# Token weights turned in two halves, and DMA-turned k copied by VectorE, in an attention and phase-MLP kernel

## The chip, the core and the metric

The kernel runs on one core of a Trainium2 chip. The metric is the device time of one execution in microseconds (us). Engines are called TensorE (PE, with its weight loads PEld), VectorE (DVE), ScalarE (ACT), GpSimd (POOL) and SyncE (SP); here SP's queue issues every DMA.

## What is computed

Two modules follow each other. The first, for 8 batches and 8 heads of 576 tokens with 64 features, adds an attention over tokens pooled by four (144 of them) to an attention in a band of seven tokens:

```python
q_d = q.reshape(B, H, Sd, factor, D).mean(axis=3)      # k_d and v_d likewise, factor 4
out_up = np.repeat(sm_attn(q_d, k_d, v_d), factor, axis=2)
mask = np.abs(pos[:, None] - pos[None, :]) < factor
scores = np.where(mask, scale * np.matmul(q, k.transpose(0, 1, 3, 2)), -1000000000.0)
return out_up + np.matmul(softmax(scores), v)
```

The second takes its result as x, with 512 features:

```python
theta = x @ w_theta
zr, zi = x * np.cos(theta), x * np.sin(theta)
y = np.einsum('ts,bsd->btd', w_tok_r, zr) + np.einsum('ts,bsd->btd', w_tok_i, zi)
u = x + y
return u + np.maximum(u @ w_ch, 0.0)
```

The token weights w_tok_r and w_tok_i are 576 by 576 each and mix tokens: output token t, input token s.

## The kernel before

The work of a batch is cut into steps, each a Python generator's turn; a string of letters, ORDER (L80), says in which order the steps of all batches are emitted, and `pin` (L683) keeps that order on every engine. A letter stands for the next step of its kind: L and v load q, k and v; C and w cast them to bf16; A turns q and k; B pools v; Q and S are pooled and band scores; N and V are pooled and local outputs; T turns the attention output to feature-major x; H gives sine and cosine of theta; Z makes z; X mixes tokens; R is the channel matmul; O is the last sum and the store. The letters l, c and W load, cast and turn the token weights (l and c the theta weights too), h and g load and cast the channel weights. D is warm-up: six matmuls of 512 columns on zeros. The letters q, t, x, z and u are DMA transposes on SP. In the text, X4.4 is step 4 of batch 4's mix, and so on.

PSUM is used as two rings: `w2` (L73) has two buffers, for q and k turns, scores and attention outputs; `w1` (L76) has four, for everything else. A step's matmuls start once the buffer's reader of two or four uses before has run.

Token weights: `weight_loads` (L220) loads five row blocks (four of 128 rows, one of 64) of w_tok_r and then five of w_tok_i. `weight_casts` (L239) casts in the same order, r on GpSimd, i on VectorE. `weight_turns` (L256) has nine steps: step j turns one block of 128 input tokens for all 576 output tokens by five TensorE transposes (the last step has ten, for the 64-token tails of r and i), and one copy of 576 columns, on ScalarE or VectorE by turns, brings it into WT.

Mix: `mix` (L615) has for each of four feature blocks dc nine matmuls of 512 columns (output tokens 0 to 511; L626) and an add on VectorE (L627), and then a tail step of 36 matmuls of 64 columns (L632) with one add (L634).

Turned q and k: for batches 6 and 7 (`DMA_QK`, L288) SP's DMA transposes turn q and k (`turn_qk`, L290), and the turned block lies in SBUF; for the others TensorE turns them into PSUM (L332). In `turns` (L315) each of the four steps of a batch then makes two copies, which also put the tokens into their order (L334): its source takes 9 tokens 128 elements apart for each run of 9 written. All are ScalarE's, but for turned k of batches 6 and 7, which GpSimd copies. VectorE pools by four after it (L342). GpSimd's other work is the casts of q, k and v (L124, L131), the band masks (L445, L447), the pooled-v product (L359), and the x sums of batches 6 and 7 (L545).

Of the kernel before, what the change touches and what calls it, by code (L numbers as in the profile page):

```python
# [9 lines left out]
FP32 = mybir.dt.float32  # L10
BF16 = mybir.dt.bfloat16
AF = mybir.ActivationFunctionType
ALU = mybir.AluOpType
AX = mybir.AxisListType

P = 128
B = 8
H = 8
S = 576
# [22 lines left out]
HALF = 64  # L42
# [5 lines left out]
def kernel(  # L48
# [11 lines left out]
    nc = tc.nc  # L60
# [15 lines left out]
    def w1(name, dt=FP32):  # L76
# [1 line left out]


    ORDER = (  # L80
        "LLLCLLCCCLLLvvvAAvKKKCLCvLCCLLlwLLDKwAwAwwSSQvSVCCBCcllCLllLQcVllNNvvvANcvwTTCCCCAcwSllllSHlccVwwVDV"
        "TTcwATAHHHZZHLSQcDcBccDSLLLLLcCCDCLvWQSZWWNzCLCLvVwCWCCvvvWWSWNZWWVLLwwwwAXVAXAvAXSSXhhBVCCNSTLuLCTT"
        "ThhgQQHVHggLLgCCVCwLHTNNHVHCCLLvXzSSZRRvvvLvwwOOZZARLALSLLRZOOAAvXCCCCwwSSXVVXANTAvvvBSXQTCLTQTCLLuL"
        "LLLCCSHVVHwvvvVHNNwwTwXAANwVHHCCCCCRSOTRQRLLLBzOOQSZZLLTTCCCvvAZRSSHHONZVXVVXNTTAZZAAwwLLwvvwHHCVHww"
        "vuLLCCCqLLSqXBXCvvSQZXNVzQCTTZCTCALLqLSSROHHNqVXVTXuTNZAALwCLCwHCqwwLLCHHSXZNVXZVXqAvvCSCBCRSSTzvvCR"
        "SROOqOSVTRQQOqTHZVVXuTVNTAHHVXNAAwwHAHRvuSSwwXwxOztXSSRVNXuQQROZSOBVRVRTOttttTORTTTSSZZRZRVxOOOXNNXH"
        "VtRVHOHHtVZHZXNZZzttVXXXXtTTuXTTTHHRHxHORRROuOZOHZzRZZOXXXXXXRRuuOROOXRRuOORORRROOO"
    )

    staged = {}  # L90
# [129 lines left out]
    def weight_loads():  # L220

        for i in range(2):
            wst = staged["w", f"th{i}"] = moep.tile([P, 1024], FP32, tag="ur", name=f"th{i}")
            nc.sync.dma_start(out=wst.rearrange("p (c e) -> p c e", c=2),
                              in_=moe_w_theta[256 * i:256 * i + 256, :].rearrange("(c p) e -> p c e", p=P))
            yield
        tail = staged["w", "tail"] = moep.tile([P, 2, S], FP32, tag="xT", bufs=2, name="tail")
        for ri, w in enumerate((moe_w_tok_r, moe_w_tok_i)):
            wst = staged["w", ri] = moep.tile([P, 4, S], FP32, tag="z", name=f"tok{ri}")
            for ct in range(5):  # L230
                nc.sync.dma_start(out=wst[:, ct, :] if ct < 4 else tail[0:OC[4], ri, :], in_=w[P * ct:P * ct + OC[ct], :])
                yield
    def channel_loads():

# [4 lines left out]
    def weight_casts():  # L239

        for i in range(2):
            gp(out=wth[:, 2 * i:2 * i + 2, :].rearrange("p c e -> p (c e)"), in_=staged.pop(("w", f"th{i}")))
            yield
        for ri in range(2):
            for ct in range(5):
                src = staged["w", ri][:, ct, :] if ct < 4 else staged["w", "tail"][0:OC[4], ri, :]
                (gp, dve)[ri](out=w_tm[ri][0:OC[ct], ct, :], in_=src)
                yield
# [6 lines left out]

    def weight_turns():  # L256

        for j in range(9):
            ps = w1(f"wps{j}", BF16)
            for ct in range(5):  # L260
                rows = OC[ct]
                for ri in ((j % 2,) if j < 8 else (0, 1)):
                    lo, n = (0, P) if j < 8 else (HALF * ri, HALF)
                    nc.tensor.transpose(
                        out=ps[lo:lo + n, ct * P:ct * P + rows],
                        in_=w_tm[ri][0:rows, ct, P * (j // 2):P * (j // 2) + n],
                        identity=ident[0:rows, 0:rows],
                    )
            (act, dve)[j % 2](out=WT[:, j, :], in_=ps[:, 0:S])
            yield  # L270

    def warm_up():

# [41 lines left out]
    def turns(b):  # L315

        q_tm, k_tm = inputs.pop(b)
        qT = work.tile([P, 4, S], BF16, tag="qT", name=f"qT{b}")
        kT = kTs[b % 2]
        qdT = work.tile([P, 4, SD], BF16, tag="qdT", name=f"qdT{b}")  # L320
        kdP = kdPs[b % 2]
        parts[b] = (qT, kT, qdT, kdP)

        for j in range(4):
            n, i = j % 2, j // 2
            tm, To = ((q_tm, qT), (k_tm, kT))[n]
            if b in DMA_QK:
                ps = turned.pop((b, j)).rearrange("p r w -> p (r w)")
            else:
                ps = w2(f"pstr{n}{i}_{b}", BF16).rearrange("p k e -> p (k e)")[:, 0:WR * P]  # L330
                for r in range(WR):
                    nc.tensor.transpose(out=ps[:, P * r:P * r + P], in_=tm[:, i, r, :, :], identity=ident)  # L332
            for a in range(2):
                (gp if b in DMA_QK and n == 1 else act)(  # L334
                    out=To[:, 2 * i + a, 0:S].rearrange("p (w r) -> p w r", r=WR),
                    in_=ps.rearrange("p (r a w) -> p a w r", r=WR, a=2)[:, a],
                )
            hs = slice(2 * i, 2 * i + 2)
            dst, src = (qdT[:, hs, :], qT[:, hs, :]) if n == 0 else (kdP[:, hs, :, 0:30], kT[:, hs, :])
            src = src.rearrange("p e (m j) -> p e m j", j=4) if n == 0 else src.rearrange("p e (g m j) -> p e g m j", g=5, j=4)  # L340
            with nc.allow_low_precision(reason="sums are taken in float32 and rounded once"):
                nc.vector.tensor_reduce(out=dst, in_=src, axis=AX.X, op=ALU.add)  # L342
            yield
# [271 lines left out]
    def mix(b):  # L615

        (xA, xB), z = parted(xTs[b]), zs.pop(b)
        uT = uTs[b] = moep.tile([P, 4 * MAIN], BF16, tag="uT", name=f"uT{b}")
        uA = uT.rearrange("p (e t) -> p e t", e=4)
        if b % 2 == 0:  # L620
            uBs[b // 2] = moep.tile([P, 4, 2, HALF], BF16, tag="uB", name=f"uB{b // 2}")
        uB = uBs[b // 2][:, :, b % 2, :]
        for dc in range(4):
            ps = w1(f"psu{dc}_{b}")
            for j in range(9):
                nc.tensor.matmul(out=ps, lhsT=z[:, j, P * dc:P * dc + P], rhs=WT[:, j, 0:MAIN], start=(j == 0), stop=(j == 8))  # L626
            nc.vector.tensor_tensor(out=uA[:, dc, :], in0=ps, in1=xA[:, dc, :], op=ALU.add)  # L627
            yield
        ps = w1(f"psut_{b}")[:, 0:4 * HALF].rearrange("p (e t) -> p e t", e=4)
        for dc in range(4):  # L630
            for j in range(9):
                nc.tensor.matmul(out=ps[:, dc, :], lhsT=z[:, j, P * dc:P * dc + P], rhs=WT[:, j, MAIN:S],  # L632
                                 start=(j == 0), stop=(j == 8))
        nc.vector.tensor_tensor(out=uB, in0=ps, in1=xB, op=ALU.add)  # L634
        yield

    def u_turn(b):
# [4 lines left out]
        if b % 2:  # L642
            utr = utrs[b // 2] = moep.tile([P, 4, P], BF16, tag="utr", name=f"utr{b // 2}")
            nc.sync.dma_start_transpose(out=utr, in_=uBs[b // 2].rearrange("p e i t -> p (e i t)"))
            yield

    rels = {}

# [89 lines left out]
```

## Time and profile before

| what | us |
|---|---|
| median of 10 runs (241.13 to 243.25) | 241.9 |
| the profiled execution's own time | 243.25 |
| its span | 241.4 |
| start of the first mix step | 50.98 |
| start of batch 3's mix | 135.75 |
| start of batch 4's mix tail | 175.50 |
| end of batch 7's last main mix step | 226.48 |
| copy of turned k on GpSimd, mean of 8 | 1.178 |
| ScalarE's table loads, 14 of | 1.283 |

The span is what the profile covers; 1.85 us of the execution's time lie outside it. A stretch is read by the busy time of each engine in it, a wait by what ended it, and the chain by following the last instruction back to what released it. A matmul's mean duration includes its pipeline; the spacing of matmuls that follow each other is the time that TensorE spends on one.

### The profile page before, as it was taken

How to read it: one execution, taken by the hardware profiler on the slowest of the kernel's cores; microseconds unless marked ns; L12 is line 12 of the kernel's file. 1: busy time of each engine (PE TensorE's matmuls, PEld its weight loads, DVE VectorE, ACT ScalarE, POOL GpSimd, SP SyncE). 2: the span in 40 equal slices, each digit the busy share in tenths (PEclk: the TensorE clock that was granted, in tenths of full speed). 3: DMA queues.
4: the chain of work that ended last, by engine and by line, in shares of the span. 5: the costliest groups of instructions: out<-in, count | busy, mean ns of one | idle time of the engine just before them, and what ended most of it. 6: DMA issues, size and time to landing. Idle time of an engine off the chain costs nothing.

```text
span 241.4 us, 6452 instructions
## 1 busy us (share of the span) xinstructions
PE 222.1 (92%) x2538; PEld 132.4 (55%) x2538; DVE 185.0 (77%) x341; ACT 158.3 (66%) x240; POOL 171.6 (71%) x231
## 2 busy tenths in 40 slices
PE   0777999999999999999999999999999999999990
PEld 0445655675576556765747556565465555445440
DVE  6355697689888988899997899889889766366552
ACT  3674889866899669899498985899772280440000
POOL 1557574998999999979849997999999954300000
PEclk9999799999999999999999999999999999999997
DMA  6999999999699999999999999989479696958296
GB/s 205 286 246 351 353 196 317 274 257 282 116 326 200 333 278 239 270 226 279 279 202 235 248 237 234 181 244 184 87 121 221 99 268 104 176 172 185 44 252 220
DMA packets 100798, 54.46 MB, mean 226 GB/s; under 512 B 85792, under 2 KB 85792, under 8 KB 100768
## 3 DMA queue, kind: packets, MB, share of 16 engines
q1 hardware_dynamic: 100768, 54.05, 96.3%
q8 instruction: 20, 0.33, 0.6%
q14 instruction: 10, 0.08, 0.1%
HBM read 33.59 MB, written 9.44 MB: 178 GB/s over the span
## 4 chain that ended last, share of the span: by engine, by line
PE 69%; POOL 12%; ACT 10%; DMA 4%; issue 2%; DVE 1%; SPq 0%; DVEq 0%; POOLq 0%; ACTq 0%
PE psu L626 22%; PE psth L562 10%; PE psr L655 7%; PE pstr L332 5%; POOL pm L445 4%; PE psloc L502 4%; POOL pm L447 4%; PE wu L277 3%; PE psS L430 3%; DMA out_dram<-osb 3%; ACT pm L438 2%; PE psut L632 2%; PE xTps L541 2%; ACT qT L334 2%; ACT kT L334 2%
## 5 line engine op out<-in xcount | busy, mean ns | idle before, releaser
L626 PE MATMUL psu<-WT,z 128*128 128x512 bf16 x288 | 66.5, 379 | 0.1
L445 POOL TENSOR_SCALAR_AFFINE_SELECT pm<-pm 128x1024 bf16<-128x1024 bf16 (+1 forms) x35 | 38.5, 1100 | 10.1 <-ACT pm L438 10.1
L438 ACT ACTIVATE pm<-psS 128x1024 bf16<-128x1024 f32 (+1 forms) x40 | 38.1, 978 | 9.6 <-PE psS L430 8.4
L626 PEld LDWEIGHTS <-z 128*128 128x128 bf16 x288 | 26.6, 98 | 29.2 <-DVE z L605 0.3
L447 POOL TENSOR_SCALAR_AFFINE_SELECT pm<-pm 128x1024 bf16<-128x1024 bf16 (+1 forms) x35 | 37.0, 1057 | 2.4
L627 DVE TENSOR_TENSOR uT<-psu,xT 128x512 bf16<-128x512 f32 x32 | 21.9, 686 | 12.5 <-PE psu L626 12.4
L562 PE MATMUL psth<-wth,xT 128*128 128x512 bf16 x128 | 31.3, 379 | 0.2 <-DVE xT L545 0.2
L655 PE MATMUL psr<-wch,uT 128*128 128x512 bf16 x128 | 31.3, 379 | 0.0
L567 ACT ACTIVATE cs<-psth,pihc 128x512 bf16<-128x512 f32 x32 | 22.4, 701 | 11.4 <-PE psth L562 9.4
L342 DVE TENSOR_REDUCE qdT<-qT 128x288 bf16<-128x1152 bf16 x16 | 21.6, 1350 | 10.4 <-ACT qT L334 10.2
L511 DVE TENSOR_TENSOR tmp<-psloc,rl 120x512 bf16<-120x512 f32 (+2 forms) x40 | 27.6, 691 | 1.4
L667 DVE SCALAR_TENSOR_TENSOR osb<-psr,ur 128x512 f32<-128x512 f32 x32 | 21.4, 685 | 7.8 <-PE psr L655 3.0
L131 POOL CAST v_w<-st_v 128x512 bf16<-128x512 f32 (+1 forms) x40 | 23.6, 612 | 5.0 <-DMA st_v<-in_v_dram 4.9
L124 POOL CAST k_tm<-st_k 128x576 bf16<-128x576 f32 x32 | 21.2, 665 | 6.3 <-DMA st_k<-in_k_dram 6.3
L342 DVE TENSOR_REDUCE kdP<-kT 128x300 bf16<-128x1200 bf16 x16 | 22.3, 1396 | 2.0 <-POOL kT L334 1.7
L334 ACT COPY qT<-pstr 128x576 bf16<-128x576 bf16 x24 | 14.2, 645 | 12.0 <-PE pstr L332 11.8
L568 ACT ACTIVATE cs<-psth 128x512 bf16<-128x512 f32 x32 | 19.5, 611 | 0.0
L124 POOL CAST q_tm<-st_q 128x576 bf16<-128x576 f32 x28 | 18.8, 671 | 0.6 <-PE pstr L332 0.6
L502 PEld LDWEIGHTS <-pm 128*128 128x128 bf16 (+1 forms) x320 | 14.9, 103 | 6.6 <-issue 1.8
L545 DVE TENSOR_TENSOR xT<-xTps,xdT 128x480 bf16<-128x480 bf16 (+3 forms) x36 | 18.4, 547 | 0.2
L334 ACT COPY kT<-pstr 128x576 bf16<-128x576 bf16 x24 | 14.4, 659 | 6.1 <-PE pstr L332 6.1
L562 PEld LDWEIGHTS <-xT 128*128 128x128 bf16 x128 | 11.5, 98 | 12.0 <-DVE xT L545 0.7
(91 smaller groups left out, 386.1 us busy)
## 6 DMA issues: line engine op xcount, KB each, us to landing
st_q<-in_q_dram SPq DMA_DIRECT2D x32, 288.0 KB, 4.8
st_k<-in_k_dram SPq DMA_DIRECT2D x32, 288.0 KB, 4.9
st_v<-in_v_dram SPq DMA_DIRECT2D x32, 256.0 KB, 6.7
out_dram<-osb SPq DMA_DIRECT2D x32, 256.0 KB, 3.3
st_v<-in_v_dram SPq DMA_DIRECT2D x8, 192.0 KB, 5.0
tok<-in_moe_w_tok_r_dram SPq DMA_DIRECT2D x4, 288.0 KB, 8.4
tok<-in_moe_w_tok_i_dram SPq DMA_DIRECT2D x4, 288.0 KB, 5.0
th<-in_moe_w_theta_dram SPq DMA_DIRECT2D x2, 512.0 KB, 8.0
```

The costliest lines, as they stand in the source:

```text
L124: eng[i](out=dst[:, hh // 2, :, hh % 2, :], in_=staged.pop((b, f"{'qk'[i]}{hh}")).rearrange("p (r d) -> p r d", d=D))
L131: gp(out=v_ws[b % 2][0:KW[c], c, :, 0:D], in_=staged.pop((b, f"v{c}"))[0:KW[c], 0:DM].rearrange("p (h d) -> p h d", d=D))
L334: (gp if b in DMA_QK and n == 1 else act)(out=To[:, 2 * i + a, 0:S].rearrange("p (w r) -> p w r", r=WR), in_=ps.rearrange("p (r a w) -> p ...
L342: nc.vector.tensor_reduce(out=dst, in_=src, axis=AX.X, op=ALU.add)
L438: nc.scalar.activation(out=pv, in_=ps[0:kw].rearrange("p e (j w) -> p (e j) w", w=P)[:, :, 0:qn], func=AF.Exp, scale=SCL,)
L445: nc.gpsimd.affine_select(out=pv, in_=pv, compare_op=ALU.is_ge, fill=0.0, base=off, pattern=[[0, 8], [-1, qn]], channel_multiplier=1)
L447: nc.gpsimd.affine_select(out=pv, in_=pv, compare_op=ALU.is_ge, fill=0.0, base=6 - off, pattern=[[0, 8], [1, qn]], channel_multiplier=-1)
L502: nc.tensor.matmul(out=pv[0:qn, h // 4, h % 4, :], lhsT=pms[b][c][0:kw, 4 * par + blk, 0:qn], rhs=v_w[0:kw, c, h, 0:65], start=(h % 4 == 0 ...
L511: nc.vector.tensor_tensor(out=tmp[0:cnt].rearrange("p (e j d) -> p e j d", e=2, j=4), in0=pv[0:cnt, :, :, 0:D], in1=rl[0:cnt].unsqueeze(3) ...
L562: nc.tensor.matmul(out=th, lhsT=xA[:, dc, P * c:P * c + P], rhs=wth[:, dc, :], start=(dc == 0), stop=(dc == 3),)
L626: nc.tensor.matmul(out=ps, lhsT=z[:, j, P * dc:P * dc + P], rhs=WT[:, j, 0:MAIN], start=(j == 0), stop=(j == 8))
L655: nc.tensor.matmul(out=psr, lhsT=uA[:, dc, P * c:P * c + P] if c < 4 else uBs[b // 2][:, dc], rhs=wch[:, dc, :], start=(dc == 0), stop=(dc ...
```

## The change

It has five parts. The loads and casts of the token weights alternate between r and i, row block by row block. The turns go by halves of the output tokens: five steps for row blocks 0 and 1 (256 tokens), then five for blocks 2 to 4 (320 tokens); a step takes two values of j (the fifth has one) into one PSUM buffer, with one copy into WT, ScalarE and VectorE by turns. Batch 0's mix (`HALVES`) takes two feature blocks and 256 output tokens in each of its four main steps, with one add per step; its tail and the other batches are as before. The copy of turned k of batches 6 and 7 goes from GpSimd to VectorE. And the ORDER string is a new one of 684 letters, as there is one turn step more; it has the same number of each other letter, among them five warm-ups, the first of which is now the first step on TensorE.

```diff
-        for ri, w in enumerate((moe_w_tok_r, moe_w_tok_i)):
-            wst = staged["w", ri] = moep.tile([P, 4, S], FP32, tag="z", name=f"tok{ri}")
-            for ct in range(5):
-                nc.sync.dma_start(out=wst[:, ct, :] if ct < 4 else tail[0:OC[4], ri, :], in_=w[P * ct:P * ct + OC[ct], :])
+        for ri in range(2):
+            staged["w", ri] = moep.tile([P, 4, S], FP32, tag="z", name=f"tok{ri}")
+        for ct in range(5):
+            for ri, w in enumerate((moe_w_tok_r, moe_w_tok_i)):
+                nc.sync.dma_start(out=staged["w", ri][:, ct, :] if ct < 4 else tail[0:OC[4], ri, :], in_=w[P * ct:P * ct + OC[ct], :])
                 yield
...
-        for ri in range(2):
-            for ct in range(5):
+        for ct in range(5):
+            for ri in range(2):
                 src = staged["w", ri][:, ct, :] if ct < 4 else staged["w", "tail"][0:OC[4], ri, :]
                 (gp, dve)[ri](out=w_tm[ri][0:OC[ct], ct, :], in_=src)
...
-        for j in range(9):
-            ps = w1(f"wps{j}", BF16)
-            for ct in range(5):
...
-            (act, dve)[j % 2](out=WT[:, j, :], in_=ps[:, 0:S])
-            yield
+        for part, cts in enumerate(((0, 1), (2, 3, 4))):
+            lo, n = 2 * P * part, sum(OC[ct] for ct in cts)
+            for k in range(5):
+                js = range(2 * k, min(2 * k + 2, 9))
+                ps = w1(f"wps{part}{k}", BF16)[:, 0:n * len(js)].rearrange("p (j t) -> p j t", t=n)
+                for j in js:
+                    for ct in cts:
...
+                (act, dve)[k % 2](out=WT[:, js[0]:js[-1] + 1, lo:lo + n], in_=ps)
+                yield
...
-                (gp if b in DMA_QK and n == 1 else act)(
+                (dve if b in DMA_QK and n == 1 else act)(
...
-        for dc in range(4):
+        for k in range(4 if b in HALVES else 0):
+            lo, dcs = 256 * (k // 2), (2 * (k % 2), 2 * (k % 2) + 1)
+            ps = w1(f"psu{k}_{b}").rearrange("p (e t) -> p e t", e=2)
+            for e, dc in enumerate(dcs):
+                for j in range(9):
+                    nc.tensor.matmul(out=ps[:, e, :], lhsT=z[:, j, P * dc:P * dc + P], rhs=WT[:, j, lo:lo + 256],
+                                     start=(j == 0), stop=(j == 8))
+            at = slice(dcs[0], dcs[1] + 1)
+            nc.vector.tensor_tensor(out=uA[:, at, lo:lo + 256], in0=ps, in1=xA[:, at, lo:lo + 256], op=ALU.add)
+            yield
+        for dc in range(0 if b in HALVES else 4):
...
+    HALVES = (0,)
```

The new order around the first mix step and around the copies of turned k, by steps, with the steps that issue only loads left out (the steps of loads, casts and DMA transposes are left out in the second):

```
before: ... W0 Q1.1 S1.2 Z0.2 W1 W2 N1.0 V1.0 W3 W4 W5 S1.3 W6 N1.1 Z0.3 W7 W8 V1.1 A2.0 X0.0
after:  ... W0 W1 Q1.0 Z0.2 B1.0 Q1.1 W2 W3 S1.2 W4 W5 V1.0 Z0.3 W6 S1.3 V1.1 W7 S1.4 N1.0 W8 A2.0 W9 N1.1 A2.1 X0.0
before: X3.0 V4.4 T4.3 X3.1 T4.4 N5.1 Z4.0 A6.1 A6.2 H4.2 H4.3 H4.4 S5.2 X3.2 Z4.1 N5.2 V5.0 X3.3 Z4.2 V5.1 X3.4 A6.3 ...
after:  X3.0 V5.0 N5.1 T4.4 X3.1 V5.1 A6.0 A6.1 A6.2 H4.1 H4.2 H4.3 H4.4 S5.2 S5.3 A6.3 X3.2 X3.3 X3.4 S5.4 Q6.0 R2.0 ...
```

## The prediction

> **What bounds the kernel now.** I read the page's busy shares and chain first, then a table of busy time in five stretches, then the tiles that the change touches. The stretches are cut where the order has landmarks: the first matmul of the mix (L626) starts at 50.98 us, the mix of batch 3 at 135.75, the 64-token tail of batch 4's mix (L632) at 175.50; the last main step of batch 7's mix ends at 226.48. Columns: us, then busy us (instructions) of TensorE, its weight loads, VectorE, ScalarE, GpSimd.
>
> ```profile
> PE 222.1 (92%) x2538; PEld 132.4 (55%) x2538; DVE 185.0 (77%) x341; ACT 158.3 (66%) x240; POOL 171.6 (71%) x231
> ...
> 0.00:50.98 50.98, 39.22 (x464) 25.23 (x465) 32.85 (x85) 36.87 (x57) 31.58 (x56) 0.97 1.00 280
> 50.98:135.75 84.77, 83.70 (x1091) 53.02 (x1089) 75.63 (x125) 70.44 (x109) 77.17 (x106) 1.00 1.09 246
> 135.75:175.50 39.75, 39.64 (x454) 22.84 (x453) 35.52 (x62) 33.15 (x45) 37.35 (x43) 1.00 0.97 205
> 175.50:226.50 51.00, 50.53 (x467) 26.93 (x464) 33.86 (x61) 17.84 (x31) 25.48 (x28) 1.00 0.79 160
> 226.50:241.40 14.90, 8.96 (x72) 4.38 (x70) 7.13 (x11) 0.00 (x0) 0.00 (x0) 0.89 0.75 204
> ```
>
> After 51 us TensorE is hardly ever free; before, it is free or in warm-up for a third of the time. In 135.75 to 175.50 three engines are nearly full at once: TensorE, GpSimd (94%) and VectorE (89%). The chain agrees: it is TensorE's but for GpSimd's pieces, of which these are in that stretch.
>
> ```profile
> 148.47 1.09 POOL pm L447
> 149.56 2.25 POOL kT L334 x2
> 151.80 0.61 POOL q_tm L124
> ...
> 218.71 7.77 PE psu L626 x36
> 226.48 2.60 PE psr L655 x12
> ```
>
> Since overlapping matmuls look busy, I count TensorE by the chain: 36 matmuls of 512 columns in 7.77 us are 0.216 us each; likewise a step of nine turns (L332) 0.50, a phase step (L562) or channel step (L655) 0.86, a band step (L430) 0.33, a mix step 1.94.
>
> **What the skill says.** Three places. (1) "SBUF — State Buffer", Who interferes with whom: a VectorE copy or cast in a two-port mode and a GpSimd instruction exclude each other for the whole instruction. The trace of before agrees: the same kind of cast takes 0.456 us while GpSimd is idle, and 1.072 us, though with half the partitions, when it begins inside a GpSimd mask; it ends 0.31 us after that mask does (41.44 + 1.10 = 42.54; 41.78 + 1.07 = 42.85).
>
> ```profile
> L247 DVE CAST wtm<-tok 128x576 bf16<-128x576 f32 x4 | 1.7, 456 | 0.5 <-DMA tok<-in_moe_w_tok_i_dram 0.5
> L247 DVE CAST wtm<-tail 64x576 bf16<-64x576 f32 x1 | 1.1, 1072 | 0.3 <-DMA tail<-in_moe_w_tok_i_dram 0.3
> ...
> 41.44 1.10 POOL L445 TENSOR_SCALAR_AFFINE_SELECT pm<-pm 128x1024 bf16<-128x1024 bf16 x1 [3.60 <-ACT pm L438]
> 41.78 1.07 DVE L247 CAST wtm<-tail 64x576 bf16<-64x576 f32 x1 [0.27 <-DMA tail<-in_moe_w_tok_i_dram]
> ```
>
> (2) "VectorE: DVE Perf Modes", Mode 2×_2P: a one-source copy from SBUF to SBUF with an even outer dimension takes this mode, whatever its strides. The casts above are such (0.456 us for 576 elements); the copy of turned k is one by its shape, 64 by 9. No row of before shows it on VectorE. (3) "SBUF — State Buffer", Specifications, Cachelines: each access that crosses to a new 16-byte line pays a penalty. The copy of turned q does so (its source steps by 128 elements), and takes 1212 ns on ScalarE against 645 for the same pattern out of PSUM:
>
> ```profile
> L334 ACT COPY qT<-pstr 128x576 bf16<-128x576 bf16 x24 | 14.2, 645 | 12.0 <-PE pstr L332 11.8
> L334 ACT COPY qT<-qk 128x576 bf16<-128x576 bf16 x8 | 9.2, 1212 | 0.0
> L334 POOL COPY kT<-qk 128x576 bf16<-128x576 bf16 x8 | 9.2, 1178 | 0.0
> ```
>
> **Loads, casts and turns of the token weights.** Bytes are the same; r and i alternate. The turns are 50 either way (9 groups of 5, and 5 more in the last, against 20 in the first half and 30 in the second); nine evictions become ten with the same 5184 columns, so one fixed cost more, a few tenths of a us on ScalarE or VectorE. That the first half is ready early buys nothing by itself: in the new order all ten turn steps stand ahead of the first mix step on TensorE. The five VectorE casts now alternate with GpSimd's; if each meets one, it costs 0.6 us more (1.07 - 0.456), 3 us of VectorE near 35 us, where ScalarE is later anyway (next step).
>
> **When the mix starts.** The new order puts one band step and one turn step more ahead of it: +0.33 + 0.50 = +0.83 us of TensorE work done early. Warm-ups are five in both; the first now runs while the first loads land, but ScalarE's q cast of the third load stands ahead of the copies of the first turned q, so the head isn't earlier. ScalarE decides: by 50.98 it has 36.9 us of work. The last turn step ahead of the new mix needs a PSUM buffer that ScalarE frees after it has done the added exp (0.78) and two copies of the step before (1.18), less some 0.3 of evictions no longer ahead: 38.5 us. With the same idle time as now, 14.1 us, that is 52.6; if no more of its 6.4 us of waits for turned q (the worst item) than a sixth goes, 51.6. I take 51.7: 0.7 us later with 0.83 us more done, so -0.1. Bounds: 1.5 earlier and 1.0 later than that.
>
> **Batch 0 by halves.** 72 matmuls of 256 columns for 36 of 512, the same columns. The 260-column ones (L470) take 0.115 in the chain's spacing where columns alone give 0.216 x 260/512 = 0.110, so 72 x 0.005 = +0.3 at most; I take +0.15. Four adds stay four of 512 elements.
>
> **The k copies, on the path.** Eight leave GpSimd (9.2 us); all eight lie between the start of batch 3's mix and the tail of batch 4's, as before. Counting steps between the landmarks in the new order: TensorE there has Q, S, B, H and R once more, one N of turns, two V and one T fewer: 0.3 + 0.33 + 0.38 + 0.86 + 0.86 - 0.26 - 0.53 - 0.21 = +1.7, so 39.75 becomes 41.5 if TensorE alone decides. (The stretches before and after give this back: -1.2 and -1.35; with +0.83 ahead they sum to nought.) VectorE has one reduce (1.37), two z (1.4), two osb (1.37) more, two V (1.78) and one T (0.65) fewer: +1.7, so 35.5 becomes 37.2 before any k copy.
> A copy costs between 0.46 (two-port, no penalty, no lock) and 1.35 ([...]the reduce's 1350/1152 being near that). I take 1.0: 0.46 of run, and a wait for GpSimd, which is still about 80% busy (37.35 - 9.2 + some 4 of steps moved in, of 41.5) with instructions of 0.6 to 1.1 us: 0.8 x 0.5 for the first of a pair, up to a whole one, 0.7 to 0.9, for the second; mean 0.55. Then VectorE needs 37.2 + 8 x 1.0 = 45.2 us. The fullest 10 us of before have it at 9.73, so 45.2/0.97 = 46.5; four PSUM buffers let TensorE be ahead by two or so VectorE instructions, -1.5: 45.0, or 3.5 over the 41.5. Queued behind a waiting copy are the adds and normalisations that free PSUM for TensorE; a copy that waits for its DMA transpose (4 us to land) now also holds these, where GpSimd held none.
>
> **The tail.** R6.3 and O6.3 stand ahead of batch 7's mix tail, so batch 6's stores are issued ahead of the last transpose (2.0 us on SP from 231.30); the last osb comes about 0.3 us earlier: -0.3.
>
> **Sum.** -0.1 + 0.15 + 3.5 - 0.3 = +3.25 on this execution's span of 241.4, or on its time of 243.25 (1.85 lies around the span). The median of the runs is 241.9; the same difference gives 245.1.
>
> **Rivals.** *TensorE covers it.* The copy is 0.46 and meets no lock: VectorE 40.9/0.97 = 42.2, less 1.5 of slack is under 41.5. Then -0.1 + 0.15 - 0.3 = -0.25: 241.6, no change. For it: the mode by the shape. Against: GpSimd is nearly always running there.
> *GpSimd's relief counts (faster).* It is the chain at 147 to 159 and 170 to 188. From 135.75 to 226.5, 90.75 us, counted TensorE work is 39.0 + 49.8 = 88.8; with 9.2 us off GpSimd the masks come earlier and up to 1.95 us of that gap goes: -2.2 with the -0.25, 239.7. It decides as long as the k copies cost VectorE under about 0.5 us each (37.2 + 4 = 41.2). Against it: recorded TensorE waits after 51 us are only 1.3 us.
> *ScalarE starts the mix late.* Copies covered, but the full 52.6 (1.6 later with 0.83 more done, +0.8) and 0.6 for the one cast that the last turns wait for: with +0.15 and -0.3 that is +1.2, 243.1. For it: ScalarE's 36.9 us of 51; against: its idle time there is waiting, which an order can move.
>
> **Chances.** VectorE becomes the bound 0.48; covered 0.10; relief 0.30; late start 0.12. What a measurement tells from no change is about 0.3% (0.7 us): faster 0.30, same 0.10, slower 0.60. The range runs from 239.3 (relief) to 248: a copy of 1.35 gives (37.2 + 10.8)/0.97 - 1.5 = 48.0, +6.3 in all, 248.2. VectorE's case alone spans 242.5 to 248.
>
> **What would show it.** The k copies' mean on VectorE near 1.0 us (wrong if under 0.6), longer when inside a GpSimd instruction; the stretch from batch 3's first mix step to batch 4's mix tail 45 us with VectorE over 95% (wrong if under 42); the first mix step at 51.7; TensorE waits on VectorE in that stretch; the end 12 us after batch 7's last main mix step. I am wrong if the copies hide, or if loads or transposes set new waits on SP.

## The result, and the profile after

The changed kernel takes 244.22 us, median of 14 runs (242.6 to 246.9), against 241.89 (240.91 to 243.68) for 51 runs of the kernel before. The ratio is 1.0075, with a 95% interval of [1.0053, 1.0096], so it is slower by about 1.8 us. The ratio leaves out executions more than 1.5% above the fastest of their kernel, so it is smaller than that of the two medians. The prediction said 245.1, in a range of 239.3 to 248.0, with 0.60 on slower.

A difference of 1.8 us is small beside what differs between executions of one kernel, so the profiled ones have to be placed first. The profiled execution of after took 242.74 us, one of its fastest; that of before took 243.25, one of its slowest. Laid side by side, the two spans (241.0 and 241.4) even show a gain of 0.4 us. Part of what follows is about that contradiction: in some executions of either kernel TensorE's granted clock falls to a half for a while in the first 35 us, and such executions are among the runs.

The landmarks of before (50.98, 135.75) were read from its chain, those of all later runs from the timeline of TensorE. The timeline has the same two matmuls of before at 50.82 and 135.59, so that before's stretch of the k copies is 39.92 us where it is set beside another run.

The page of after, its busy shares; then its table of busy time in the prediction's five stretches, cut at the same landmarks (columns: us, then busy us and instructions of TensorE, its weight loads, VectorE, ScalarE and GpSimd; granted clock, DMA share, GB/s).

```profile
PE 221.2 (92%) x2574; PEld 135.7 (56%) x2574; DVE 191.7 (80%) x349; ACT 157.9 (66%) x241; POOL 163.8 (68%) x223
```

```profile
0.00:51.36 51.36, 40.10 (x480) 24.94 (x481) 34.02 (x85) 38.16 (x61) 33.23 (x59) 0.97 1.03 282
51.36:134.19 82.83, 81.68 (x1119) 56.19 (x1117) 74.03 (x125) 66.86 (x104) 76.71 (x105) 1.00 1.06 251
134.19:177.50 43.31, 41.59 (x458) 23.67 (x456) 41.92 (x71) 35.74 (x48) 33.00 (x40) 1.00 1.02 199
177.50:226.69 49.19, 48.97 (x455) 26.58 (x452) 34.35 (x60) 17.19 (x30) 20.85 (x23) 1.00 0.72 153
226.69:241.00 14.31, 8.82 (x72) 4.37 (x70) 7.34 (x11) 0.00 (x0) 0.00 (x0) 0.99 0.76 211
```

The third row is the stretch of the eight k copies: 43.31 us where before took 39.92, with VectorE now busy for 41.92 of it (97%) and GpSimd for only 33.00 (76%). The second and fourth rows gave 1.9 and 1.8 us back.

The view of the tile that holds the DMA-turned blocks says what a copy costs now (count, then shortest, median and longest in ns):

```profile
L339 DVE COPY kT<-qk x8: 647/655/1535, 141.9 to 171.7; 128x576 bf16<-128x576 bf16 x8
```

Six of the eight take 0.65 us and two far more; the mean is 0.830. The chain of after, in order of time, runs through VectorE at two places of the stretch:

```profile
144.50 1.34 DVE qdT L347
145.84 0.33 DVE zT L587
146.18 1.16 DVE kT L339 x2
147.35 1.42 DVE kdP L347
...
165.54 1.26 DVE qdT L347
166.80 1.15 DVE kT L339 x2
167.97 1.40 DVE kdP L347
```

The copies (L339) stand between the pooling reduces (L347) of q and k with no pause: a reduce, the two copies and the next reduce follow each other, and TensorE waits behind them. The chain of before had GpSimd's pieces there.

### The profile page after: what moved, and what is told of

Read it like the earlier page. It is cut to its first block, busy times and chain, and to the rows that moved or that the text cites. A ratio compares the mean times of both kernels' runs of the same rounds, so it can differ in the third digit from the quotient of the medians.

```text
span 241.0 us, 6532 instructions
## 1 busy us (share of the span) xinstructions
PE 221.2 (92%) x2574; PEld 135.7 (56%) x2574; DVE 191.7 (80%) x349; ACT 157.9 (66%) x241; POOL 163.8 (68%) x223
## 4 chain that ended last, share of the span: by engine, by line
PE 56%; DVE 16%; DMA 13%; POOL 6%; ACT 4%; issue 3%; SPq 0%; DVEq 0%; POOLq 0%
PE psu L641 17%; PE psr L672 8%; PE psth L567 7%; DMA out_dram<-osb 5%; DMA tok<-in_moe_w_tok_r_dram 4%; PE psu L633 3%; DMA st_v<-in_v_dram 3%; PE psloc L507 3%; PE pstr L337 3%; PE psS L435 2%; DMA st_q<-in_q_dram 2%; PE psut L647 2%; PE xTps L546 2%; DVE osb L684 2%; DVE qdT L347 2%
## 5 line engine op out<-in xcount | busy, mean ns | idle before, releaser
L641 PE MATMUL psu<-WT,z 128*128 128x512 bf16 x252 | 57.6, 379 | 0.2 <-DVE osb L684 0.2
L641 PEld LDWEIGHTS <-z 128*128 128x128 bf16 x252 | 23.7, 98 | 26.5 <-issue 0.2
L672 PE MATMUL psr<-wch,uT 128*128 128x512 bf16 x128 | 30.8, 379 | 0.9 <-DVE uT L642 0.9
L347 DVE TENSOR_REDUCE qdT<-qT 128x288 bf16<-128x1152 bf16 x16 | 21.6, 1348 | 8.0 <-ACT qT L339 7.8
L642 DVE TENSOR_TENSOR uT<-psu,xT 128x512 bf16<-128x512 f32 x28 | 18.8, 687 | 9.3 <-PE psu L641 9.3
L347 DVE TENSOR_REDUCE kdP<-kT 128x300 bf16<-128x1200 bf16 x16 | 22.4, 1399 | 1.3 <-ACT kT L339 1.1
L339 ACT COPY qT<-pstr 128x576 bf16<-128x576 bf16 x24 | 14.3, 654 | 8.0 <-PE pstr L337 7.9
L672 PEld LDWEIGHTS <-uT 128*128 128x128 bf16 x128 | 11.5, 98 | 13.1 <-issue 1.2
```

What stands on the lines that cost most here:

```text
L672: nc.tensor.matmul(out=psr, lhsT=uA[:, dc, P * c:P * c + P] if c < 4 else uBs[b // 2][:, dc], rhs=wch[:, dc, :], start=(dc == 0), stop=(dc ...
```

## The experiments

Three theories were put to the test. A: the eight k copies make VectorE the bound of the stretch from batch 3's mix to batch 4's mix tail, and that is the loss. B: the loss is in the head, where the first mix step comes later (B1: because two steps, a band step S1.4 and a turn step A2.1, were put ahead of it). C: the VectorE copies alone are the loss, and GpSimd has room for them, so that they should go back. Each ratio below is to runs of the kernel before on the same chip beside it.

### The changed kernel once more

> The changed kernel once more, to see what differs from one execution to the next: its times reach from 242.6 to 246.9 us where the kernel before has 240.9 to 243.7. Theory A (VectorE is the bound from batch 3's mix to batch 4's mix tail, owing to the k copies): that stretch is again 43.3 us, within 0.5, and the ratio is 1.0075 again. Rival B (the loss is in the head, ahead of the first mix step, where TensorE is often free and its clock falls): the stretch from there on is the same and the first mix step comes at another time than 51.4 us, 1 to 4 us later in a slow execution, with more half-clock time.

Measured: 243.42 us, median of 22 (242.63 to 247.19), ratio 1.0058 [1.0033, 1.0083]. Of the 22, seven took 244.7 to 247.2 with a mean granted clock of 0.983 or less; the other fifteen took 242.6 to 245.1, most of them under 243.4. The profiled execution (242.63) had its first mix step at 51.06 and no half-clock period ahead of it. The stretch of the copies was 43.33 us again, as A expected.

### The copies back on GpSimd, in the new order

```diff
-                (dve if b in DMA_QK and n == 1 else act)(
+                (gp if b in DMA_QK and n == 1 else act)(
```

> The changed kernel with the eight copies of turned k back on GpSimd, all else and the order as changed. Theory A: VectorE loses 6.6 us in the stretch from batch 3's mix to batch 4's mix tail and GpSimd gets 9.4, so GpSimd's 33.0 us become 42.4 of 43.3; the stretch is then bound by GpSimd, 42 to 44 us, and the time stays within 1 us of the changed kernel's. Rival B (the head): no part of the loss is in the copies, the time is the changed kernel's plus what GpSimd now delays, 0 to 2 us more. Rival C (the VectorE copies alone are the loss, GpSimd has room): 1.5 us or more faster than the changed kernel.

Measured: 248.6 us (248.38 to 251.49), ratio 1.0292 [1.0246, 1.0337]: worse than every theory allowed. The stretch took 49 us. Its row in the table of stretches, then two of the waits there (us in all, times, longest) and the copies that TensorE's wait goes back to:

```profile
137.54:186.56 49.02, 42.02 (x451) 24.10 (x455) 37.32 (x64) 35.84 (x48) 39.74 (x47) 0.93 0.91 177
```

```profile
PE psSd L387 <- DVE kdP L347: 6.3, 1, 6.3
...
POOL pm L450 <- ACT pm L443: 2.5, 1, 2.5
```

```profile
154.48 2.23 POOL L339 COPY kT<-qk 128x576 bf16<-128x576 bf16 x2
```

VectorE is busy for 37.32 us, what the prediction had worked out for it without the copies (37.2). But TensorE once waits 6.3 us for the pooled k, which waits for GpSimd's copies of k. These start only at 154.48: in GpSimd's order they stand behind four masks, the first of which had waited 2.5 us for ScalarE. So C falls: in the new order GpSimd has no room where the copies stand, and they cost 5 us more there than on VectorE (248.6 against 243.42), though the whole change is a loss. The expectation under A was wrong too: it took GpSimd's free time as if it could be used at any moment.

### A dearer copy on VectorE

The same 576 elements, read along the source and written with steps.

```diff
-                    out=To[:, 2 * i + a, 0:S].rearrange("p (w r) -> p w r", r=WR),
-                    in_=ps.rearrange("p (r a w) -> p a w r", r=WR, a=2)[:, a],
+                    out=To[:, 2 * i + a, 0:S].rearrange("p (w r) -> p r w", r=WR),
+                    in_=ps.rearrange("p (r a w) -> p a r w", r=WR, a=2)[:, a],
```

(for the eight k copies alone)

> The changed kernel, but each k copy on VectorE runs along its source (64 tokens side by side, nine times) and scatters its writes, where it ran along its destination. If the reads that step by 128 elements are what makes the undisturbed copy 0.65 us, it falls to about 0.4 us (VectorE's casts of 576 elements take 0.456), and VectorE has 2 us less to do in the stretch from batch 3's mix to batch 4's mix tail. Theory A: that stretch falls from 43.3 to about 41.5 us and the time by 1.5 us. Rival B (the head): the stretch may fall but the time changes by less than 0.5 us.

Measured: 252.61 us (251.62 to 254.92), ratio 1.0434 [1.0396, 1.0473]. The expectation about the copy failed: it became dearer, not cheaper. Its tile view and its stretch:

```profile
L340 DVE COPY kT<-qk x8: 1549/1824/2464, 141.6 to 181.0; 128x576 bf16<-128x576 bf16 x8
```

```profile
133.90:188.13 54.23, 44.91 (x451) 25.34 (x456) 50.64 (x72) 35.88 (x48) 41.14 (x42) 0.91 0.79 161
```

It serves A all the same: more of the same load in the same place. A copy of 1.93 us in place of 0.83 puts 8 x 1.10 = 8.8 us more on VectorE, and the stretch grows by 54.23 - 43.31 = 10.9. Some 2 us of that may be a consequence: TensorE, now waiting, had its clock halved for a part of the stretch (0.91).

### Before's order, with the copies on VectorE

```diff
-                (gp if b in DMA_QK and n == 1 else act)(
+                (dve if b in DMA_QK and n == 1 else act)(
```

(an edit of the kernel before)

> The kernel before with this one part of the change: k copies of batches 6 and 7 on VectorE, order as before. Theory A: VectorE's 35.5 us of the 39.75 us between batch 3's mix and batch 4's mix tail become 42 or more (eight copies at 0.65 to 1.2 us), so the stretch becomes 42 to 44 us and the time 2 to 4 us longer than before. Rival B (the copies cost nothing, the head is the loss): within 1 us of the kernel before.

Measured: 247.03 us (245.07 to 247.82), ratio 1.0189 [1.015, 1.0228], or 4.6 us. Two stretches of it:

```profile
49.17:134.28 85.11, 83.04 (x1077) 53.01 (x1090) 76.01 (x126) 70.39 (x109) 77.86 (x106) 1.00 1.09 247
134.28:179.51 45.23, 41.35 (x454) 23.55 (x458) 42.06 (x69) 33.91 (x45) 31.58 (x38) 0.96 0.94 184
```

Both the stretch and the time came out longer than A expected (42 to 44 us, and 2 to 4 us), and far from B's forecast of no cost. The stretch that was 39.92 is 45.23. So the copies alone cost 5.3 us there in the old order (up to 1.7 of it through a half-clock period of 3.4 us, the 0.96, while TensorE waits); the new order, which puts 1.7 us more TensorE work into the stretch, brings it to 43.31. This run gives a second thing: its head is before's, instruction for instruction, and here the first mix step starts at 49.17, not at 50.82.

### The head: when the mix starts, and the clock

The kernel before was profiled with a half-clock period at about 23 to 27 us. The same time in the repeated changed kernel and in the one with the copies on GpSimd, which have the same head (busy times as above; the number after GpSimd's is the granted clock):

```profile
20.00:25.00 5.00, 3.76 (x66) 2.50 (x62) 3.51 (x9) 1.36 (x3) 5.00 (x9) 1.00 1.05 386
25.00:30.00 5.00, 4.14 (x67) 3.69 (x67) 4.73 (x9) 3.97 (x8) 3.31 (x5) 1.00 1.07 384
30.00:35.00 5.00, 4.90 (x26) 1.99 (x25) 5.00 (x10) 4.97 (x9) 1.53 (x2) 1.00 0.99 178
```

```profile
20.00:25.00 5.00, 3.68 (x49) 2.57 (x48) 3.19 (x9) 1.60 (x4) 4.58 (x8) 0.71 1.05 394
25.00:30.00 5.00, 5.00 (x56) 4.18 (x55) 3.40 (x7) 1.63 (x3) 4.06 (x6) 0.50 1.06 391
30.00:35.00 5.00, 4.78 (x44) 3.78 (x44) 4.08 (x7) 4.40 (x9) 1.17 (x2) 0.77 1.19 218
```

These are the same instructions, and in one execution the clock is full, in the other halved for (0.29 + 0.50 + 0.23) x 5 us x 2 = 10.2 us. Its first mix step starts at 54.71, against 51.06. The Trainium skill, "TensorE: Matmul & The Clock Gate", Part 1 (The HAM clock gate), describes a monitor that halves TensorE's clock after an idle window of some 3.4 us; the periods in these heads are 3.4 us (before and after) or three times that (10.2 here), so the length agrees. But TensorE was not idle for so long here: it was busy for 3.7 of 5 us in both executions, and one of them was throttled. What decides between the two is not shown.

*A sixth warm-up* ahead of the local-output step V0.1, in ORDER:

```diff
-LLLVVNN
+LLLDVVNN
```

> The changed kernel with a sixth warm-up (six matmuls of 512 columns on zeros, 1.3 us) ahead of the second local output of batch 0, at about 20 us, where TensorE waits 0.9 us. Theory B's part on the clock: the half-clock periods between 20 and 33 us, which come in some executions only, are owed to TensorE being too idle at 13 to 24 us; they go or become rarer, no execution has a mean clock under 0.985, and the mean of all falls by about 1 us while the fastest stay at 242.6 or become 0.5 us longer. If the clock periods have another cause: as many executions at 246 as now, all 0.4 us longer.

Measured: 243.5 us (243.41 to 243.84), ratio 1.0057 [1.0042, 1.0072]. By the mean clock (0.993 or more) none of its six executions had a long half-clock period, nor had any of the 22 of the run without copies below, which has the same head: 28 of 28, where the changed kernel had 15 of 22 free of one. On the same chip as these six, nine of 25 executions with the head of the changed kernel (the runs with before's rest and without halves) had a clock of 0.977 or less. The first mix step comes at 51.99, 0.9 later, and the fastest execution is slower by 0.8 (243.41 against 242.63). So half-clock periods are a cost in some executions, and the cure costs the others as much as it saves on the whole: the ratio is that of the changed kernel.

*The two steps behind the first mix step*, in ORDER:

```diff
-WSNWAWNALXV
+WNWAWNLXASV
```

> The changed kernel with two steps moved: the last band step of batch 1 and the second turn step of batch 2 stand right behind the first mix step instead of ahead of it. Theory B1 (these two make the mix wait for ScalarE: the turn needs a PSUM buffer that ScalarE empties after the exp and two copies): the first mix step comes at 49.3 to 50 us instead of 51.1, with 0.83 us less done, so the time falls by about 0.8 us in executions with an equal clock; the executions at 246 stay. Rival B2 (the loads, casts and turns themselves are late): first mix step at 50.3 or later, no gain in time.

Measured: 245.23 us (243.09 to 247.58), ratio 1.0111 [1.0068, 1.0154]; five of its nine executions had a clock of 0.982 or less. TensorE's timeline around the first mix steps (L633), of the repeated changed kernel and then of this one (start, us, and in brackets the idle time ahead and what ended it):

```profile
50.55 0.68 PE L337 MATMUL pstr<-ident,k_tm 128*128 128x128 bf16 x9 [0.58 <-POOL k_tm L124]
51.06 2.13 PE L633 MATMUL psu<-WT,z 128*128 128x256 bf16 x18
...
53.78 2.13 PE L633 MATMUL psu<-WT,z 128*128 128x256 bf16 x18
```

```profile
49.37 2.22 PE L633 MATMUL psu<-WT,z 128*128 128x256 bf16 x18
...
53.36 0.41 PE L507 MATMUL psloc<-v_w,pm 128*128 128x65 bf16 x8 [0.96 <-ACT kT L339]
54.54 1.69 PE L633 MATMUL psu<-WT,z 128*128 128x256 bf16 x14
```

B1 is right that these two steps hold the first mix step back (49.37) and wrong about what this is worth and about the engine. In the changed kernel the turn step waits 0.58 us for GpSimd's cast of k, not for ScalarE. Behind the first mix step the two steps bring another wait, 0.96 us for ScalarE's copy, the second mix step comes at 54.54, not 53.78, and no time is gained: the fastest execution takes 243.09, against 242.63.

*Before's head with the new rest.* The weight loads, casts and turns as before, ORDER of before up to the first mix step and of after from there, the copies on VectorE; the two steps S1.4 and A2.1, which before's head leaves out, stand right ahead of the first mix step.

```diff
-ORDER: head of after ... WSNWAWNA + rest of after
+ORDER: head of before ... ZWWVLLwwwwAhvvSA + rest of after
```

> Head as before (loads, casts and turns of the token weights, and the order up to the first mix step), everything after it in the new order, with the k copies on VectorE; batch 0's mix as before. Theory B (the head is what costs; what follows the first mix step is about 0.8 us shorter than before, 189.6 against 190.4, less 0.83 of steps that the new head had done early): the first mix step at 49.2 us in an undisturbed execution, the time within 1 us of the kernel before, 241.5 to 242.5, and few executions above 244. Theory A (the copies are the net loss): 243 or more, as the changed kernel.

Measured: 243.97 us (242.51 to 247.31), ratio 1.0063 [1.0036, 1.009]: as slow as the changed kernel, where 241.5 to 242.5 was expected. The first mix step starts at 51.68, with no half clock ahead of it. The splice carried the two steps along, and they hold it back here too, behind another engine: the band step waits 0.89 us for VectorE. So the late start needs neither the halves nor the alternating loads.

*The new head with before's rest*, the copies on GpSimd as before:

```diff
-ORDER: head of after ... WSNWAWNA + rest of after
+ORDER: head of after ... WSNWAWNA + rest of before
-                (dve if b in DMA_QK and n == 1 else act)(
+                (gp if b in DMA_QK and n == 1 else act)(
```

> The reverse: the changed head (token weights by halves, new order up to the first mix step), then batch 0's mix by halves and the order of before with the k copies on GpSimd. Theory B: the first mix step at 51.1 us, or 54.7 when the clock is halved for 10 us ahead of it; the time 242.5 to 243.5 as the changed kernel, with a share of executions at 246. Theory A: the loss goes with the copies, 241.5 to 242.3.

Measured: 243.75 us (243.28 to 247.07), ratio 1.008 [1.004, 1.0119], three of ten executions with a clock of 0.976 or 0.977. Its stretches:

```profile
0.00:51.07 51.07, 39.43 (x481) 24.66 (x481) 33.95 (x85) 38.05 (x61) 33.22 (x59) 1.00 1.02 283
51.07:136.31 85.24, 83.21 (x1112) 55.83 (x1110) 75.88 (x125) 68.84 (x106) 75.85 (x104) 1.00 1.05 244
136.31:176.27 39.96, 39.83 (x459) 22.94 (x456) 35.54 (x62) 33.36 (x45) 37.99 (x44) 1.00 1.04 200
```

The stretch of the copies is before's again (39.96). With none of the copies on VectorE its ratio is that of the changed kernel, so A alone, which expected 241.5 to 242.3, is not enough. But not all of this is the head. At full clock the first mix step comes 51.07 - 49.17 = 1.9 us later, with 0.83 us of work done early, and the second stretch is longer than before's (85.24 against 84.77) although it has that work less to do. So the head costs about 1.1 us, and the stretch behind it, where the two orders are joined, about as much. B holds beside A, and the two together would be more than was measured, if the new order did not give time back elsewhere. The gain of 2 us between the first mix step and batch 3's mix belongs to the new order of that stretch, not to the head: the run with before's head and the new rest has 83.04 us there.

### The halves

```diff
-    HALVES = (0,)
+    HALVES = ()
```

> The changed kernel with batch 0's mix as before (36 matmuls of 512 columns instead of 72 of 256), order unchanged. If halving costs what 0.005 us a matmul gives, the time falls by 0.1 to 0.4 us, within the noise of the changed kernel; if the halves serve the mix (its start waits for the second half's turns otherwise), it becomes longer by more than 0.5 us. The first mix step stays at 51.1 us in an execution without half clock ahead of it.

Measured: 244.23 us (242.5 to 246.33), ratio 1.0072 [1.0038, 1.0106], that of the changed kernel. Batch 0's mix by halves costs nothing that can be measured. (The profiled execution has a half-clock period in its head and starts the mix at 51.51; what the expectation said of the start without one was not seen.) It shows something else: in this execution none of the eight k copies had to wait for a GpSimd instruction, and the stretch is 0.8 us shorter than in after.

```profile
L339 DVE COPY kT<-qk x8: 647/652/661, 142.0 to 171.2; 128x576 bf16<-128x576 bf16 x8
```

```profile
134.24:176.75 42.51, 41.43 (x459) 23.70 (x456) 41.12 (x71) 35.63 (x48) 31.74 (x40) 1.00 1.00 207
```

The other way round, before's order with the new loads, casts and turns and the halves, the copies on GpSimd, did not isolate them:

```diff
-ZWWVLL
+ZWWWVLL
```

> The order of before with the changed token weights only: loads and casts that alternate between r and i, turns by halves with the tenth turn step right behind the ninth, batch 0's mix by halves; k copies on GpSimd. Theory B1 (the order of the head costs, the halves do not): within 0.7 us of the kernel before, the first mix step at 49.2 to 49.6 us in an undisturbed execution (51 with one half-clock period ahead of it). Rival B2 (the halves cost): the first mix step at 50.5 us or later without half clock, 1 us or more longer.

Measured: 253.64 us (252.4 to 255.88), ratio 1.0472 [1.0434, 1.051], with the first mix step at 60.83. The timelines of VectorE and GpSimd say why:

```profile
45.56 1.29 DVE L610 TENSOR_TENSOR z<-psxt,cs 128x1024 bf16<-128x1024 bf16 x2 [7.04 <-DMA st_k<-in_k_dram]
```

```profile
44.86 0.66 POOL L248 CAST wtm<-tok 128x576 bf16<-128x576 f32 x1
```

VectorE sat for 7.04 us ahead of z. The view names a load as the releaser, but z begins just when GpSimd's cast of the last 128-row block of w_tok_r ends (44.86 + 0.66 = 45.52), and z takes the buffer from which that cast reads (both have the tag "z", which has two buffers), so the cast and not the load released it. With alternating loads in the old order, SP issues that block's load only at 33.20 us, where before had issued it by 24.4, and its cast comes behind two masks. Both forecasts failed: the old order has no place for alternating loads, and what halves and alternation cost apart in the old order stays open.

### The copies shared, and left out

One copy of each pair on VectorE, the other on GpSimd:

```diff
-                (dve if b in DMA_QK and n == 1 else act)(
+                ((dve, gp)[i] if b in DMA_QK and n == 1 else act)(
```

> The changed kernel with the k copies of the first turned block of batches 6 and 7 on VectorE and of the second on GpSimd. Theory A (VectorE sets the stretch from batch 3's mix to batch 4's mix tail, 43.3 us with 97% of VectorE busy): VectorE loses 3.3 us there, GpSimd's 33 become 38: the stretch falls to 41.5 to 42.5 us and the time by about 1 us. If GpSimd's place in the order is what matters (it does worse than its sum, as in the run with all eight copies back on it, where the stretch was 49.0), the stretch becomes 45 us or more and the time 2 us longer.

Measured: 249.83 us (248.59 to 251.18), ratio 1.0329 [1.0293, 1.0365]. A's forecast failed; the other came true by more than it said. The stretch, and the longest wait of VectorE in it:

```profile
134.11:184.57 50.46, 42.93 (x458) 24.27 (x456) 40.66 (x67) 35.85 (x48) 36.50 (x43) 0.93 0.88 174
```

```profile
153.29 1.40 DVE L347 TENSOR_REDUCE kdP<-kT 128x300 bf16<-128x1200 bf16 x1 [7.20 <-POOL kT L339]
```

VectorE stands idle for 7.20 us until GpSimd, behind its masks as in the run with all eight copies there, has made the first two of its own. Later GpSimd stands for 3.9 us until a DMA transpose of k has landed, and then its copies and VectorE's fall on each other: in the mean the four on VectorE take 1.158 us and those on GpSimd 1.346.

Last, the kernel with the sixth warm-up, once with the eight copies and once without. It leaves the reordering copy of turned k out for batches 6 and 7, which then use an older k.

```diff
-            for a in range(2):
-                (dve if b in DMA_QK and n == 1 else act)(
+            for a in range(0 if b in DMA_QK and n == 1 else 2):
+                act(
```

> The kernel with the sixth warm-up (243.5 us, 243.4 to 243.8, no half clock), with the eight copies of turned k of batches 6 and 7 left out: those batches use k of earlier ones. Nothing takes their place on another engine. Theory A (VectorE sets the stretch from batch 3's mix to batch 4's mix tail, now 43.3 us, TensorE's own work there being 41.5): VectorE falls from 41.9 us to 35.5, the stretch to 41.5 to 42 us, and the time to 241.5 to 242.2. Rival (the stretch is long for another reason, such as the order of loads and transposes): the stretch stays above 42.8 and the time above 243.

Measured: 241.04 us, median of 22 (240.45 to 241.78), ratio 0.9962 [0.9949, 0.9975], against 1.0057 [1.0042, 1.0072] with the copies. The stretch with the copies and without:

```profile
134.81:178.11 43.30, 41.59 (x458) 23.68 (x456) 41.91 (x71) 35.72 (x48) 33.04 (x40) 1.00 0.98 199
```

```profile
135.06:176.15 41.09, 41.06 (x458) 23.56 (x456) 37.31 (x64) 35.70 (x48) 30.80 (x39) 1.00 1.07 214
```

The copies cost 2.2 us in the stretch and 2.5 us of the whole time. Without them TensorE is busy for 41.06 of 41.09 us: it alone sets the stretch, and VectorE has 37.31 (35.5 had been expected; the prediction's 37.2 was nearer). Leaving a copy out also takes away its wait for the DMA transpose, but in the run with the copies no VectorE instruction of the stretch waits for a transfer, so that is not what was saved. That shows A, and it is the one version faster than before, by less than what is left out. Among the kernels that compute everything, none beat the kernel before.

## Why the prediction was right, and where it was off

The sign, the place and the mechanism were right: VectorE, once it has the k copies, becomes the bound between batch 3's mix and batch 4's mix tail. The predicted difference was +3.25 us and the measured one 1.8. That the whole came out slower is in part luck: the new order gave back more than half of what the copies cost, and much of the loss that was measured belongs to the head and to half-clock executions, which the prediction's sum had at about nothing. Step by step:

| step of the sum | predicted, us | measured, us |
|---|---|---|
| first mix step starts at | 51.7 | 51.36; 51.06 in the repeat |
| that against before, work done early counted | -0.1 | -0.3 with one half-clock period in each head; +1.1 with none |
| halves | +0.15 | +0.1 (a step 1.97 in the chain, for 1.94) |
| TensorE alone, stretch of the copies | 41.5 | 41.09 |
| VectorE without the copies | 37.2 | 37.3 |
| a k copy on VectorE, mean | 1.0 | 0.830 |
| stretch of the copies | 45.0 | 43.31 |
| so, on the path | +3.5 | +1.8 to +2.2 |
| tail | -0.3 | -0.6, but not owed to the order |
| gains of the order elsewhere, work counted | none | -1.2 |

**The copies.** The term that was mis-sized is the copy. I took 0.46 us of run and 0.55 of wait for GpSimd; it is 0.65 of run and 0.17 of wait. The run was too short because I priced it by a cast that reads its source in order. The Trainium skill, "VectorE: DVE Perf Modes", Mode 2×_2P, names no condition on the strides for this mode, but the same number of elements takes 0.65 us in place of 0.456 when the source steps by 128 elements; this difference, 0.2 us, is of the kind that "SBUF — State Buffer", Cachelines, names, though no run here changes the step alone.

The wait was too long because I multiplied occupancies. GpSimd is busy for 76% of the stretch, near the 80% that I assumed, but six of the eight copies began while it stood idle, four during a wait for a load and two during a wait for ScalarE. Where they do meet, both lose, as the timelines of GpSimd and VectorE in after show:

```profile
169.03 0.61 POOL L131 CAST v_w<-st_v 128x512 bf16<-128x512 f32 x1 [3.80 <-DMA st_v<-in_v_dram]
170.14 1.09 POOL L450 TENSOR_SCALAR_AFFINE_SELECT pm<-pm 128x1024 bf16<-128x1024 bf16 x1 [0.49 <-ACT pm L443]
171.30 1.40 POOL L452 TENSOR_SCALAR_AFFINE_SELECT pm<-pm 128x1024 bf16<-128x1024 bf16 x1
172.65 1.02 POOL L131 CAST v_w<-st_v 96x512 bf16<-96x512 f32 x1
```

```profile
166.72 1.21 DVE L339 COPY kT<-qk 128x576 bf16<-128x576 bf16 x2
...
170.55 2.64 DVE L339 COPY kT<-qk 128x576 bf16<-128x576 bf16 x2
```

The pair at 166.72 falls into GpSimd's 3.80 us of waiting for v and takes 1.21 us together. The pair at 170.55 begins inside a mask (170.14 + 1.09) and takes 2.64; the masks and the cast that alternate with it take 1.40 in place of 1.09 and 1.02 in place of 0.61. With the measured copy my own formula gives (37.2 + 8 x 0.83)/0.97 - 1.5 = 43.7, and 43.31 was measured. It fits two other executions of the new order as well: with copies of 0.652 us (the run without halves) it gives 42.2, and 42.51 was measured; with 0.913 (the run with before's head) 44.4, and 44.00. So the formula held and its input did not. In the old order it doesn't hold: 35.7 us of VectorE and copies of 0.867 give 42.5, and 45.23 was measured. TensorE shows most of the cost as waits for VectorE; in the stretch of after these are

```profile
PE psr L672 <- DVE uT L642: 0.9, 1, 0.9
PE psS L435 <- DVE kT L339: 0.4, 1, 0.4
...
PE psSd L387 <- DVE kdP L347: 0.3, 1, 0.3
```

or 1.6 us of the 1.8 to 2.2. The longest is for an add (uT) that frees PSUM: VectorE works without a pause from the slow pair of copies at 170.55 up to it.

**The head.** The start was forecast well in number (51.7, measured 51.1 to 51.4), but by the wrong wait, so that was luck. The prediction let ScalarE decide when the last turn step ahead of the mix can start. In the chain of after this step follows GpSimd, and from 40 us on the chain is GpSimd's, but for short pieces of issue:

```profile
47.98 1.06 POOL pm L450
...
49.09 1.09 POOL pm L452
50.18 0.62 POOL k_tm L124
...
50.85 0.68 PE pstr L337 x9
```

From 40 to 51 us GpSimd is busy for 10.75 of 11.00 us. ScalarE's copy that the step could wait for ends at 50.48, 0.3 us before GpSimd's cast of k (50.79). The effect was misjudged too. I compared the start with before's profile, which has a half-clock period in its head; the same head at full clock starts the mix at 49.17. With 0.83 us of work done early the changed kernel loses 51.06 - 49.17 - 0.83 = 1.1 us there, near what the rival of the late start had (0.8), beside the main case and not in its place, and not for its reason.

**The gains that I left out.** From the first mix step to batch 3's mix the time fell from 84.77 to 82.83, of which the work moved is 1.2; from batch 4's mix tail to the end of the last main mix step from 50.97 to 49.19, of which 1.35. That is 0.7 and 0.4 us of true gain. That the gain of the second stretch belongs to its order is shown by the two runs that join one kernel's head to the other's rest (85.24 and 83.04); which wait went is not: no run took that order apart. Nor does a run show whether GpSimd's relief had a part in these gains. The tail's 0.6 us is no gain of the order: with before's rest behind the new head the tail is 14.34 us, as short as in after (14.31).

**The clock.** Not foreseen at all. In the repeat, the seven executions with a mean clock of 0.983 or less have a median of 246.49 us, the other fifteen of 243.24; the one trace with so long a period (10.2 us) starts its mix 3.65 us later than the repeat. Of before's 27 runs beside them, eight have the mean clock of its profiled execution (0.985 or 0.986), which had a period of 3.4 us in its head; their median is 243.18, against 242.09 for the rest. At full clock in the head the two kernels are thus about 1 us apart: 243.24 - 242.09 = 1.15 by these groups, and 0.95 by the spans (240.7 for the repeat, and for before 241.4 less the 50.82 - 49.17 = 1.65 of its period). The table's measured column gives the same: 1.1 - 1.2 + 1.7 - 0.6 = 1.0, with 1.7 for the repeat's own stretch (43.33 - 39.92, less 1.7 of moved work). The rest of the 1.8 would come from half-clock executions; this is an estimate from the groups, and no run separates it, since the sixth warm-up removes the long periods but costs 0.9 us itself. Executions near full clock differ too (242.6 to 245.1 in the repeat). One such trace, of the run with before's head (245.52), has copies of 0.913 us, a stretch of 44.00 and a tail of 15.79; why its tail is longer stays open.

**A slip.** The prediction's last part has the end 12 us after batch 7's last main mix step; its own tail term gives 14.9 - 0.3 = 14.6, and 14.31 was measured. And 45.2/0.97 is 46.6, not 46.5.

## What to carry to other kernels

When a step moves to another engine, price the stretch in which all its instances lie, by that engine's busy time there plus the moved work, and ask for the engine's occupancy at the places where they fall rather than in the mean. An order is made for its engines: here the copies cost 5.3 us of a stretch on VectorE in the old order and 2.2 in the new one, where on GpSimd they cost more still. When a start comes out where it was forecast, look at the wait that ends there: here the number was right and the engine was not. And before a profile is used as the base of a sum, set its time beside the median and look at the granted clock: 1.35 us above the median was here nearly as much as the effect itself.

## What the runs showed of the hardware that was not expected

- A VectorE copy of 128 x 576 bf16 within SBUF takes 0.65 us with a source that steps by 128 elements and a dense destination, and 1.55 to 2.46 us with a source read along and a destination that steps by 9 elements. The element count and the types are the same. How much of the second range is waiting for GpSimd was not separated.
- TensorE's clock was halved for 3.4 or 10.2 us in a head where it was busy for about three quarters of the time, and by the mean clock the long periods came in seven of 22 executions of one and the same kernel, and in none of 28 once one more warm-up stood there.
- A GpSimd mask that alternates with VectorE copies takes 1.40 us in place of 1.09, while the two copies take 2.64 in place of 1.21: both engines lose.
